# A written order for all engines, and attention products in four array quadrants, in a fused attention and gated-conv kernel

## Chip, cores and metric

The kernel runs on one NeuronCore of a Trainium2 chip. The metric is the device time of one execution in microseconds (us). Before the change the median of 3 runs is 379.87 us (379.6 to 380.04).

## What is computed

Windowed attention for 4 batches, 8 heads, 768 positions of 64 values feeds a two-layer block with a gate. In the reference, cut to what matters:

```python
k_sum = k.reshape(B, H, nb, 32, D).max(axis=3)      # 24 summary keys
v_sum = v.reshape(B, H, nb, 32, D).mean(axis=3)     # 24 summary values
scores_l = scale * q @ k.T, only where |i - j| < 16
scores_s = scale * q @ k_sum.T + log(32)
a = softmax(concat(scores_l, scores_s))
x = a @ concat(v, v_sum)                            # 4 x 768 x 512 over all heads
h = relu(x @ w_in)                                  # 512 -> 1024
conv_out = 3 taps along the sequence, per channel, of h
out = (h * sigmoid(conv_out)) @ w_out               # 1024 -> 512
```

All of it is in 32-bit floats. The two large products are made from split operands: a high part and a low part of each, three products of four (high-high, high-low, low-high).

## The kernel before

The sequence of each batch is cut into two halves, so there are 8 chunks c of 384 positions. Two heads make a pair, so a chunk has 4 pairs, and the program 32, counted n. A pair has 6 blocks of 64 queries; a block sees 96 keys of its own window and the 24 summary keys, 120 in all.

For a pair, `qk` (line 303) makes the scores: TensorE multiplies 64x64 queries with 64x120 keys, two heads in the two halves of the array's rows, two blocks in the two halves of its columns, so four run at once. `softmax` adds the mask and finds the maximum on VectorE (`masked`, 349), takes six exponentials on ScalarE (`expo`, 366), the reciprocal on VectorE (`recip`), and scales on GpSimd (`norm`). The probabilities are turned on TensorE, from pair SPLIT = 14 on by `turn_both` (417), 64 rows at a time into two PSUM banks, and copied out by ScalarE. `av` (441) multiplies 120 keys with 64 queries: the two heads stand in the two halves of the array's columns, and each takes all of its rows. A product of 32-bit floats is two matmul records, so `av` has 24. Its result in PSUM bank x is split into xh (cast by ScalarE) and xl (subtraction by VectorE, `x_lo`).

For a chunk, `f1` (538) projects x to 128 channels at a time, unit u of 8, with 12 matmuls. `relu` and `tap_mid` follow on ScalarE or VectorE (ScalarE for the chunks in TAP_ACT, VectorE for the middle taps of the others), `taps` on VectorE, `gate_tanh` on ScalarE, `gate_prod` on VectorE, `gate_hi` mostly on ScalarE, `gate_lo` on GpSimd. `f2` (641) contracts the gated channels into output tiles, three matmuls per piece; `f2_out` (667) copies a tile out on ScalarE, which also issues its store.

In the first half of a batch, each pair also needs its summaries: `key_max` and `val_sums` reduce on VectorE, `val_turn` (276) turns the sums on TensorE into bank x, `val_mean` (284) scales them on ScalarE, `load_vm` brings them behind the other values by a DMA, and `key_sums` (263) copies the summary keys behind the window on GpSimd. The tiles kw, q and va have 3, 4 and 4 buffers.

The order: chunks 0 and 1 and the pairs up to 13 follow the string ORDER, which holds on TensorE, VectorE, GpSimd and SyncE, and on ScalarE by added dependencies. From chunk 2 on `unit` (789) traces the work of one projection, and only TensorE keeps the traced order:

```python
    with tc.manual_schedule(engines={every.PE}):
        for c in range(FIRST, NCHUNK):
            pieces = work(c)
            for u in range(NFC):
                unit(c, u, pieces)
```

The framework's scheduler places the work of the other engines, and may place it ahead of the end of ORDER. In odd units, `unit` traces on TensorE the transposes of pair m-1, the scores of m and the products of m-2, then `f1`, then the pieces of `f2`; even units have `f1`, pieces, and in the first half of a batch `val_turn` ahead of them. The PSUM banks are: x; t for transposes; two banks s for scores; f2; and three for `f1`, of which one is given to the transposes at pair 15.

Of the kernel before, what the change touches and what calls it, by code (L numbers as in the profile page):

```python
# [18 lines left out]
P = 128  # L19
# [69 lines left out]
def attention_ffn(ctx, tc, qT, kT, vT, v4, w_in, cwT, w_out, mask8, ident_in, out):  # L89
# [98 lines left out]


    state = {}  # L190
    banks = ["f1a", "f1b", "f1c"]

    def f1_bank(name):
# [20 lines left out]
    def load_k(n):  # L214
        b, p = divmod(n // (2 * NP) * NP + n % NP, NP)
        tag, bufs = ("kw", 3) if 2 <= n < NP else ("kT", 2)
        k = sp.tile([P, SP], F32, tag=tag, name=f"k{n}", bufs=bufs)
        nc.sync.dma_start(k, kT[b, p])
        of(n)["k"] = k

    def load_kw(n):
        c, p = divmod(n, NP)
        b, hf = divmod(c, 2)
        first = kT[b, p, :, hf * CH : hf * CH + WK]
        nc.sync.dma_start(kw_tile(n)[:, :, :WK], window(first, 1, [SP, P], WK))

    def load_vt(n):
        c, p = divmod(n, NP)
        if c == 0:
            v = raw_b[:, 2 + p, :S].bitcast(F32)  # L230
        else:
            v = sp.tile([P, 1024], F32, tag="stage", name=f"vt{n}", bufs=2)[:, :S]
        nc.sync.dma_start(v, vT[c // 2, p])
        of(n)["vt"] = v

    def load_q(n):
        c, p = divmod(n, NP)
# [16 lines left out]
    def load_vm(n):  # L254
        nc.sync.dma_start(of(n)["va"][WK:NK, :, :], vm_wide(n))
# [37 lines left out]
    def first_half(n):  # L293
        return n // NP % 2 == 0
# [71 lines left out]
    def expo(n, h, i):  # L366
        st = of(n)
        this = nc.scalar.activation(  # L368
            st["a", h][:, i, :],
            st["a", h][:, i, :],  # L370
            AF.Exp,
            bias=st["nm"][:, h, i : i + 1],
            scale=-1.0,
            accum_out=st["acc"][:, h, i : i + 1],
        )
        before = st.setdefault("expos", [])
        if n >= NP:
            for x in before:
                tc.declare_no_dep(
                    ins(this), ins(x), reason="one engine, sums in columns of their own"  # L380
                )
        before.append(this)

    def recip(n):
        st = of(n)
# [8 lines left out]
    def softmax(n):  # L394
        for h in range(2):
            for i in range(3):
                masked(n, h, i)
            for i in range(3):
                expo(n, h, i)
        recip(n)  # L400
        for h in range(2):
            norm(n, h, "g")
# [6 lines left out]
        of(n)["pt", h] = pt  # L409

    def turned(n, h, eng):
        aT = sp.tile([P, 3 * P], F32, tag="aT", name=f"aT{n}_{h}", bufs=4)
        copy(eng, aT[:NK, :], of(n)["pt", h][:NK, : 3 * P])
        for blk in range(CB):
            of(n)["aT", h, blk] = aT[:NK, blk * QB : (blk + 1) * QB]

    def turn_both(n):
        st = of(n)
        a = [st.pop(("a", h)) for h in range(2)]
        pt = [  # L420
            ps.tile([P, 512], F32, tag=tag, name=f"pt{n}_{tag}") for tag in ("t", *given)
        ]
        for h in range(2):
            for i in range(3):
                at = (h * 3 + i) * QB
                for half in range(2):
                    r = slice(half * QB, (half + 1) * QB)
                    nc.tensor.transpose(  # L428
                        pt[half][:NK, at : at + QB], a[h][r, i, :], ident[r, r]
                    )  # L430
        for half in range(2):
            aT = sp.tile([P, 3 * P], F32, tag="aT", name=f"aT{n}_b{half}", bufs=4)
            nc.scalar.copy(aT[:NK, :], pt[half][:NK, : 3 * P])
            for h in range(2):
                for i in range(3):
                    at = (h * 3 + i) * QB
                    st["aT", h, 2 * i + half] = aT[:NK, at : at + QB]
# [3 lines left out]
    def av(n):  # L441
        st = of(n)
        xp = ps.tile([P, 512], F32, tag="x", name=f"xp{n}")
        for blk in range(CB):
            for h in range(2):
                r = slice(h * QB, (h + 1) * QB)
                nc.tensor.matmul(  # L447
                    xp[r, blk * QB : (blk + 1) * QB],
                    st["va"][:NK, blk, r],
                    st["aT", h, blk],  # L450
                    start=True,
                    stop=True,
                )
        st["xp"] = xp

    def x_tiles(c):
        xT[c] = [
# [20 lines left out]
        xh, xl = x_at(n)  # L478
        nc.vector.tensor_tensor(xl, of(n)["xp"][:, :CH], xh.bitcast(F32), ALU.subtract)  # L479

    npair = NCHUNK * NP

    def slot(j):

        if j % 2 == 0:
            n = j // 2 + 2
            if n < npair:
                if first_half(n):
                    load_k(n)
                load_kw(n)  # L490
                if first_half(n):
                    load_vt(n)
            n = j // 2
            if n < npair:
                load_vm(n)
                qk(n)
                softmax(n)
        else:
            n = (j + 1) // 2
            if n + 1 < npair:  # L500
                load_q(n + 1)
            if n < npair:
                if first_half(n):
                    val_sums(n)
                    val_turn(n)
                    val_mean(n)
                load_v(n)
                if first_half(n):
                    key_max(n)
                key_sums(n)  # L510

    def turn_one(j):
        n, h = divmod(j, 2)
        turn(n, h)
        turned(n, h, "s")

    def slot_t(j):
        if j % 2 == 0 and j - 2 < NGROUP and j // 2 - 1 >= SPLIT:
            turn_both(j // 2 - 1)

    def slot_av(j):
        n = j - 4
        if n % 2 == 0 and n < NGROUP:
            n //= 2
            c, p = divmod(n, NP)
            av(n)
            if p == 0:
                x_tiles(c)
                if c % 2:
                    x_edge(c)  # L530
            xh, xl = x_at(n)
            nc.scalar.copy(xh, of(n)["xp"][:, :CH])
            x_lo(n)


# [200 lines left out]
        mybir.DependencyClass.NoSync, mybir.DependencyReason.DATA  # L736
    )

    def run(order):
        traced = nc.cur_bb.bb.instructions  # L740
        front, behind, of_exp = [], [], None
        for token in order.split():
            what, at, eng = re.fullmatch(r"([a-zA-Z]+)([\d.]*)(?:/([svg]))?", token).groups()
            args = [int(x) for x in at.split(".") if x]
            start = len(traced)
            steps[what](*args, *([eng] if eng else []))
            for x in traced[start:]:
                if x.engine != every.Activation:
                    continue
                exp = args[0] if what == "e" else None  # L750
                if exp is None or exp != of_exp:
                    front, behind, of_exp = [], front, exp
                for y in behind:
                    tc.add_manual_dep(x, y.name, order_only, reason="order")
                front.append(x)

    with tc.manual_schedule(engines={every.PE, every.DVE, every.Pool, every.SP}):
        run(ORDER)
# [13 lines left out]
        parts = [(*t, [fc]) for t in tiles for fc in range(NFC)]  # L772
        return deal(parts, (3, 3, 2, 3, 3, 2, 4, 4))

    pending = []
    given, spare = [], [banks[0]]

    def gates(lag):

        while len(pending) > lag:  # L780
            c, fc = pending[0]
            b, hf = divmod(c, 2)
            old = (0, 1, 2) if hf == 0 else (2, 3, 4, 5)
            if b and not all((b - 1, st, fc) in contracted for st in old):
                return
            pending.pop(0)
            gate_mul(c, fc)

    def unit(c, u, pieces):

        j = 8 * (c + 1) + 3 + u
        if j == 2 * SPLIT + 2:
            given.append(banks.pop(banks.index(spare[0])))
        early = divmod(j - 2, 2)[0]
        if early < SPLIT and j % 2 == 0:
            turn_one(j - 2)
        slot_t(j)
        slot(j)
        slot_av(j)
        if early < SPLIT:  # L800
            if j % 2 == 0:
                turn_one(j - 1)
            elif u == 0:
                turn_one(j - 2)
        gates(1)
        f1(c, u, range(NCC))
        gate_conv(c, u)
        pending.append((c, u))
        assert len(pending) <= 2
        for x in pieces[u]:  # L810
            f2(*x)
        if c == NCHUNK - 1:
            gates(0)

    with tc.manual_schedule(engines={every.PE}):
        for c in range(FIRST, NCHUNK):
            pieces = work(c)
            for u in range(NFC):
                unit(c, u, pieces)

    banks += given
    for st in (2, 3, 4):
# [63 lines left out]
```

## Time and profile before

| | |
|---|---|
| median of 3 runs | 379.87 us |
| the profiled execution | 379.0 us, its span 376.9 us |
| TensorE matmuls busy | 368.7 us, 98% |
| VectorE busy | 251.7 us, 67% |
| ScalarE busy | 241.9 us, 64% |
| GpSimd busy | 145.2 us, 39% |

PE is TensorE's matmul, PEld its weight load, DVE VectorE, ACT ScalarE, POOL GpSimd. Times of rows count from the start of the span. Matmuls overlap, so a busy PE may still have room; what a matmul costs is read from the distance between starts. In a timeline a row starts with its start and its length in us, "xN" is a count of merged instructions, and brackets tell of idle time before it and what ended it.

### The profile page before, as it was taken

What the parts mean: (1) busy time and instruction counts of PE and PEld (TensorE: products, weight loads), DVE (VectorE), ACT (ScalarE), POOL (GpSimd) and SP (SyncE); (2) the same over time, 40 slices, a digit from 0 to 9 for tenths busy, and PEclk for the clock granted to TensorE, in tenths of its full rate; (3) what the DMA queues carried; (4) which work ended last, traced back from release to release, by engine and by line L of the source; (5) the groups of instructions that cost most, each with busy time, mean ns of one, the idle gap of its engine ahead of it and who ended that gap; (6) DMA issues with size and microseconds to landing.
All of it is one profiled execution on the core that took longest, in us unless ns stands there. A gap on an engine that the chain in (4) does not pass through costs nothing.

```text
span 376.9 us, 9285 instructions
## 1 busy us (share of the span) xinstructions
PE 368.7 (98%) x3407; PEld 319.6 (85%) x3407; DVE 251.7 (67%) x786; ACT 241.9 (64%) x770; POOL 145.2 (39%) x178
## 2 busy tenths in 40 slices
PE   8988999999999999999999999999999999999996
PEld 6767798888878888888888888888888988999886
DVE  3999999999877566786755655566756655565200
ACT  2999989997577677675656777665656643334211
POOL 0656577877245333423424334324323322222200
PEclk9999999999999999999999999999999999999999
DMA  7999899797974554662232442442120000000011
GB/s 288 370 330 297 230 274 319 224 248 203 277 265 149 136 161 139 175 197 72 73 103 83 121 122 85 125 115 56 64 67 3 30 28 13 16 30 28 28 57 56
DMA packets 42365, 53.27 MB, mean 141 GB/s; under 512 B 21520, under 2 KB 30160, under 8 KB 42320
## 3 DMA queue, kind: packets, MB, share of 16 engines
q1 hardware_dynamic: 38432, 46.14, 42.1%
q10 hardware_dynamic: 3888, 6.54, 4.9%
q8 instruction: 27, 0.44, 0.5%
q14 instruction: 18, 0.15, 0.2%
HBM read 44.31 MB, written 6.29 MB: 134 GB/s over the span
## 4 chain that ended last, share of the span: by engine, by line
PE 83%; DVE 8%; ACT 5%; issue 2%; DMA 1%; DVEq 0%; ACTq 0%
PE f L549 33%; PE f L654 32%; PE xp L447 5%; PE pq L318 5%; PE pw L115 2%; PE pt_t L428 2%; DVE t L590 2%; PE f L687 2%; ACT a L368 1%; DVE wu L139 1%; DMA wo<-w_out 1%; DVE wl L133 1%; PE pt L408 1%; DVE a L355 1%; ACT wu L122 1%
## 5 line engine op out<-in xcount | busy, mean ns | idle before, releaser
L629 POOL TENSOR_TENSOR glo<-t,ghi 128x383 fp32r<-128x383 f32 (+1 forms) x64 | 65.0, 1017 | 117.7 <-ACT ghi L147 108.9
L549 PE MATMUL f<-xh,win_hi 128*128 128x384 f32 (+1 forms) x256 | 92.0, 359 | 2.0 <-DVE t L611 1.9
L590 DVE SCALAR_TENSOR_TENSOR t<-f,cw,t 128x384 f32<-128x384 f32 (+3 forms) x128 | 78.4, 616 | 14.2 <-ACT t L577 10.9
L549 PE MATMUL f<-xl,win_hi 128*128 128x384 f32 (+1 forms) x256 | 86.8, 339 | 0.0
L549 PE MATMUL f<-xh,win_lo 128*128 128x384 f32 (+1 forms) x256 | 86.5, 338 | 0.0
L368 ACT ACTIVATE a<-a,nm 128x120 f32<-128x120 f32 x192 | 68.9, 400 | 9.9 <-DVE nm L355 8.7
L654 PE MATMUL f<-wout_hi,ghi 128*128 128x512 f32 x184 | 72.4, 394 | 0.0
L654 PE MATMUL f<-wout_lo,ghi 128*128 128x512 f32 x184 | 72.1, 392 | 0.0
L654 PE MATMUL f<-wout_hi,glo 128*128 128x512 f32 x184 | 71.6, 390 | 0.0
L606 ACT ACTIVATE t<-t 128x385 f32<-128x385 f32 (+1 forms) x64 | 33.7, 527 | 57.0 <-DVE t L590 56.3
L392 POOL TENSOR_TENSOR a<-a,sm 128x360 f32<-128x360 f32 x59 | 46.4, 803 | 54.9 <-DVE sm L387 52.3
L549 PEld LDWEIGHTS f<-xh,win_hi 128*128 128x128 f32 x256 | 48.2, 188 | 8.0 <-DVE t L611 3.9
L611 DVE SCALAR_TENSOR_TENSOR t<-t,f 128x383 f32<-128x383 f32 (+1 forms) x64 | 35.3, 552 | 29.4 <-ACT t L606 29.2
L549 PEld LDWEIGHTS f<-xl,win_hi 128*128 128x128 f32 x256 | 48.4, 189 | 1.4 <-DVE xl L479 0.3
L549 PEld LDWEIGHTS f<-xh,win_lo 128*128 128x128 f32 x256 | 48.3, 189 | 0.0
L355 DVE CUSTOM_DVE_ANT_0 a<-pq,mask 128x120 f32<-128x120 f32 x192 | 42.3, 277 | 3.3 <-PE pq L331 1.7
L654 PEld LDWEIGHTS f<-wout_hi,glo 128*128 128x128 f32 x184 | 34.5, 188 | 7.5
L567 ACT ACTIVATE f<-f 128x384 f32<-128x384 f32 (+1 forms) x63 | 30.8, 491 | 15.3 <-PE f L549 14.8
L654 PEld LDWEIGHTS f<-wout_hi,ghi 128*128 128x128 f32 x184 | 34.6, 188 | 5.6 <-ACT ob L669 0.3
L654 PEld LDWEIGHTS f<-wout_lo,ghi 128*128 128x128 f32 x184 | 34.6, 188 | 4.9
L368 ACT ACTIVATION_READ_ACCUMULATOR a<-a,nm 128x1 f32 x192 | 33.8, 176 | 0.0
L147 ACT CAST ghi<-t 128x383 fp32r<-128x383 f32 (+1 forms) x58 | 30.0, 517 | 5.9 <-DVE t L611 5.6
(76 smaller groups left out, 491.0 us busy)
## 6 DMA issues: line engine op xcount, KB each, us to landing
va<-v SPq DMA_DIRECT2D x32, 288.0 KB
kw<-kT SPq DMA_DIRECT2D x24, 288.0 KB
k<-kT SPq DMA_DIRECT2D x16, 400.0 KB
q<-qT SPq DMA_DIRECT2D x32, 192.0 KB
out_dram<-ob ACTq DMA_DIRECT2D x23, 256.0 KB
vt<-vT SPq DMA_DIRECT2D x12, 384.0 KB
wo<-w_out SPq DMA_DIRECT2D x8, 512.0 KB
raw_a<-w_in SPq DMA_DIRECT2D x6, 512.0 KB
```

The lines of the kernel that those rows point to most:

```text
L147: nc.scalar.copy(out, x)
L318: nc.tensor.matmul(pq[h][half * QB : (half + 1) * QB, i * NK : i * NK + keys.shape[-1]], st["q"][r, blk * QB : (blk + 1) * QB], keys, star ...
L355: nc.vector.tensor_tensor_reduce(st["a", h][:, i, :], st["pq"][h][:, i * NK : (i + 1) * NK], mask[:, edge(n, i), :], -0.125, 3.0e38, ALU.a ...
L368: this = nc.scalar.activation(st["a", h][:, i, :], st["a", h][:, i, :], AF.Exp, bias=st["nm"][:, h, i : i + 1], scale=-1.0, accum_out=st[" ...
L392: by[eng].tensor_tensor(a, a, s, ALU.mult)
L549: nc.tensor.matmul(ph[:, :n], w[:, fc, cc, :], x[:, cc, :n], start=(cc == 0 and m == 0), stop=(cc == NCC - 1 and m == 2),)
L567: nc.scalar.activation(h[:, :n], h[:, :n], AF.Relu)
L590: nc.vector.scalar_tensor_tensor(t[:, i0:i1], h[:, hf + k - 1 + i0 : hf + k - 1 + i1], cw[:, fc, k : k + 1], t[:, i0:i1], ALU.mult, ALU.add,)
L606: nc.scalar.activation(t, t, AF.Tanh, scale=0.5)
L611: nc.vector.scalar_tensor_tensor(t, t, 1.0, h[:, hf : hf + ng], ALU.add, ALU.mult)
L629: nc.gpsimd.tensor_tensor(gate_at("lo", c, fc), t, hi.bitcast(F32), ALU.subtract)
L654: nc.tensor.matmul(po, gx[:, fc, ss], w[:, fc, :], start=(fc == 0 and m == 0), stop=(fc == NFC - 1 and m == 2),)
```

## The change

From chunk 2 on `row` (odd units) and `between` (even units) write the order for TensorE, VectorE, GpSimd and SyncE, and `in_order` extends ScalarE's ordering to it. In a row TensorE now has the scores of pair m, the products of m-2, the transposes of m-1, the projection, the pieces. From pair 13 on the products are cut (`av_halves`): 64 keys go to bank x, the other 56 to free columns of three other banks, so that four products of 64x64 stand in the four quadrants of the array. ScalarE copies the first part out (`x_first`), VectorE adds the second to it (`x_sum`), GpSimd casts and subtracts. The tiles of turned probabilities have 3 buffers instead of 4. Reductions, gates and copies have fixed places. `slot`, `slot_t`, `slot_av`, `gates` and `unit` go.

```diff
+    def av_halves(n):
+        st = of(n)
+        xp = ps.tile([P, 512], F32, tag="x", name=f"xp{n}")
+        if n + 2 < npair:
+            last = of(n + 2)["pq"][1]
...
+        for blk in range(CB):
+            i, half = divmod(blk, 2)
+            if half == 0:
+                parts.append(rest[i][:, 3 * P :])
+            for k, keys in enumerate((slice(0, QB), slice(QB, NK))):
+                for h in range(2):
+                    r = slice(h * QB, (h + 1) * QB)
+                    at = blk * QB if k == 0 else half * QB
+                    nc.tensor.matmul(
+                        (parts[i] if k else xp)[r, at : at + QB],
+                        st["va"][keys, blk, r],
+                        st["aT", h, blk][keys, :],
+                        start=True,
+                        stop=True,
+                    )
+        st["x0"], st["parts"] = xp, parts
+
+    def x_first(n):
+        xs = sp.tile([P, DM], F32, tag="wl", name=f"xs{n}", bufs=1)[:, :CH]
+        nc.scalar.copy(xs, of(n)["x0"][:, :CH])
+        of(n)["xp"] = xs
+
+    def x_sum(n):
+        xs = of(n)["xp"]
+        for i, more in enumerate(of(n)["parts"]):
+            at = xs[:, i * P : (i + 1) * P]
+            nc.vector.tensor_tensor(at, at, more, ALU.add)
...
+    def x_rows(n, eng):
...
+        copy(eng, xh, of(n)["xp"][:, :CH])
+        if eng == "g":
+            nc.gpsimd.tensor_tensor(xl, of(n)["xp"], xh.bitcast(F32), ALU.subtract)
+        else:
             x_lo(n)
...
+    def row(c, u, before):
+        m = (8 * (c + 1) + 3 + u) // 2
+        new = m > SPLIT
...
+        here = m < npair
+        n = m + 2
+        if n < npair:
+            if first_half(n):
+                load_k(n)
+            load_kw(n)
+            if first_half(n):
+                load_vt(n)
+        if not new:
+            turn_one(2 * m - 2)
+        if here:
+            load_vm(m)
+            qk(m)
+        if m - 2 < npair:
+            if new:
+                av_halves(m - 2)
+            else:
+                av(m - 2)
+        if new and m - 1 < npair:
+            turn_both(m - 1)
+        gate_tanh(*before)
+        if here:
+            masks(m, 0)
+        gate_prod(*before)
+        if here:
+            masks(m, 1)
+        if new and m - 2 < npair:
+            x_first(m - 2)
+        gate_hi(*before, "s")
+        gate_lo(*before)
+        if not new:
+            x_rows(m - 2, "s")
+            turn_one(2 * m - 1)
+        if here:
+            expos(m, 0)
+            expos(m, 1)
+        if new and m - 2 < npair:
+            x_sum(m - 2)
+            x_rows(m - 2, "g")
+        if new and m - 1 < npair:
+            turned_both(m - 1)
+        if here:
+            recip(m)
+            for h in range(2):
+                norm(m, h, "g")
         f1(c, u, range(NCC))
+        relu(c, u, "s")
+        mid(c, u)
+        n = m + 1
+        if n < npair:
+            if first_half(n):
+                key_max(n)
+                val_sums(n)
+            key_sums(n)
+        taps(c, u)
+
+    def between(c, u, before):
+        m = (8 * (c + 1) + 4 + u) // 2
+        if c == FIRST and u == 0:
+            turn_one(2 * m - 3)
+            key_sums(m)
+        if m + 1 < npair:
+            load_q(m + 1)
+        if m < npair:
+            load_v(m)
+        if before:
+            gate_tanh(*before)
+            gate_prod(*before)
+        f1(c, u, range(NCC))
+        relu(c, u, "s")
+        mid(c, u)
+        if before:
+            gate_hi(*before, "s")
+            gate_lo(*before)
+        if m < npair and first_half(m):
+            val_turn(m)
+            val_mean(m)
+        taps(c, u)
+
+    before = ()
+    with tc.manual_schedule(engines={every.PE, every.DVE, every.Pool, every.SP}):
+        start = len(nc.cur_bb.bb.instructions)
         for c in range(FIRST, NCHUNK):
             pieces = work(c)
             for u in range(NFC):
-                unit(c, u, pieces)
+                (row if u % 2 else between)(c, u, before)
+                for x in pieces[u]:
+                    f2(*x)
+                before = (c, u)
+        gate_mul(*before)
+        in_order(start)
```

## Rows read from the trace of the kernel before

**Rows 1.** Busy time by stretch: PE, PEld, DVE, ACT, POOL busy, clock, DMA share, GB/s

```profile
120.00:300.00 180.00, 180.00 (x1734) 157.41 (x1733) 116.91 (x387) 119.53 (x394) 64.22 (x82) 1.00 0.36 102
```

**Rows 2.** Waits of TensorE: in total, times, longest; the first row

```profile
PE f L549 <- DVE t L611: 1.9, 3, 0.9
```

**Rows 3.** Chain that ended last, in time, from the scores of pair 22 to those of 26

```profile
196.67 0.78 PE pq L318 x24
...
200.59 2.06 PE f L654 x9
202.65 2.10 PE f L549 x12
...
239.60 0.78 PE pq L318 x24
```

**Rows 4.** PE timeline, narrow stretches of pair 22; products by line (ns min/median/max)

```profile
196.75 0.59 PE L318 MATMUL pq<-kw,q 64*64 64x120 f32 x16
...
197.16 0.28 PE L318 MATMUL pq<-kw,q 64*64 64x120 f32 x4
197.38 0.28 PE L447 MATMUL xp<-aT_b,va 120*64 120x64 f32 x2
...
197.48 0.40 PE L447 MATMUL xp<-aT_b,va 120*64 120x64 f32 x8
...
L447 PE MATMUL xp<-aT_b,va x24: 222/222/270, 197.4 to 198.1; 120*64 120x64 f32 x24
```

**Rows 5.** PE timeline in two narrow stretches: scores of 96 columns, pair 0

```profile
6.07 0.40 PE L318 MATMUL pq<-k,q 64*64 64x96 f32 x8
...
6.07 0.48 PE L318 MATMUL pq<-k,q 64*64 64x96 f32 x12
```

**Rows 6.** Masks by line (busy us, mean ns); ACT and DVE timeline, pair 22

```profile
L355 DVE CUSTOM_DVE_ANT_0 a<-pq,mask 128x120 f32<-128x120 f32 x192 | 42.3, 277 | 3.3 <-PE pq L331 1.7 <-PE pq L318 1.3
...
197.04 0.46 ACT L433 COPY aT_b<-pt_t 120x384 f32<-120x384 f32 x1
...
197.77 0.52 ACT L147 CAST ghi<-t 128x383 fp32r<-128x383 f32 x1
198.43 0.40 ACT L368 ACTIVATE a<-a,nm 128x120 f32<-128x120 f32 x1
...
200.46 0.55 ACT L532 CAST xh<-xp 128x384 fp32r<-128x384 f32 x1
...
203.40 0.52 ACT L606 ACTIVATE t<-t 128x383 f32<-128x383 f32 x1 [1.34 <-DVE t L590]
...
202.10 1.27 DVE L590 SCALAR_TENSOR_TENSOR t<-f,cw,t 128x382 f32<-128x382 f32 x2 [0.50 <-ACT t L577]
203.96 0.55 DVE L611 SCALAR_TENSOR_TENSOR t<-t,f 128x383 f32<-128x383 f32 x1 [0.59 <-ACT t L606]
```

**Rows 7.** Timeline around the end of ORDER: ACT, DVE, POOL, PE

```profile
105.13 0.48 ACT L567 ACTIVATE f<-f 128x386 f32<-128x386 f32 x1 [0.20 <-issue]
...
108.19 2.71 DVE L590 SCALAR_TENSOR_TENSOR t<-f,cw,t 128x382 f32<-128x382 f32 x5 [1.60 <-ACT t L577]
...
87.86 0.30 POOL L265 COPY kw<-ks 128x144 f32<-128x144 f32 x1
...
112.87 0.51 POOL L149 CAST ghi<-t 128x385 fp32r<-128x385 f32 x1
113.46 1.02 POOL L629 TENSOR_TENSOR glo<-t,ghi 128x385 fp32r<-128x385 f32 x1
...
109.31 0.84 PE L318 MATMUL pq<-kw,q 64*64 64x120 f32 x24
...
112.36 0.44 PE L549 MATMUL f<-xh,win_hi 128*128 128x384 f32 x1 [0.88 <-DVE t L611]
```

**Rows 8.** Groups by line: reduction of keys, copy of the value means

```profile
L260 DVE TENSOR_REDUCE ks<-k 128x24 f32<-128x768 f32 x16 | 15.1, 945 | 5.1 <-DMA k<-kT 4.6 <-POOL kw L265 0.5
...
L287 ACT ACTIVATE vm<-pv 24x128 f32<-24x128 f32 x16 | 4.0, 258 | 4.2 <-PE pv L281 4.2
```

More of the change, by code (lines that the diff above doesn't have):

```diff
@@ L190, in attention_ffn @@
     state = {}
+    of_exps = {}
     banks = ["f1a", "f1b", "f1c"]
@@ L382, in expo @@
         before.append(this)
+        of_exps[ins(this).name] = n
     def recip(n):
@@ L411, in turned @@
     def turned(n, h, eng):
-        aT = sp.tile([P, 3 * P], F32, tag="aT", name=f"aT{n}_{h}", bufs=4)
+        aT = sp.tile([P, 3 * P], F32, tag="aT", name=f"aT{n}_{h}", bufs=3)
         copy(eng, aT[:NK, :], of(n)["pt", h][:NK, : 3 * P])
@@ L415, in turned, with turned_banks @@
             of(n)["aT", h, blk] = aT[:NK, blk * QB : (blk + 1) * QB]
+    def turned_banks(n):
+        st = of(n)
+        if "pts" not in st:
+            st["pts"] = [
+                ps.tile([P, 512], F32, tag=tag, name=f"pt{n}_{tag}")
+                for tag in ("t", *given)
+            ]
+        return st["pts"]
     def turn_both(n):
@@ L419, in turn_both @@
         a = [st.pop(("a", h)) for h in range(2)]
-        pt = [
-            ps.tile([P, 512], F32, tag=tag, name=f"pt{n}_{tag}") for tag in ("t", *given)
-        ]
+        pt = turned_banks(n)
         for h in range(2):
@@ L430, in turn_both, with turned_both @@
                     )
+    def turned_both(n):
+        st = of(n)
+        pt = st["pts"]
         for half in range(2):
-            aT = sp.tile([P, 3 * P], F32, tag="aT", name=f"aT{n}_b{half}", bufs=4)
+            aT = sp.tile([P, 3 * P], F32, tag="aT", name=f"aT{n}_b{half}", bufs=3)
             nc.scalar.copy(aT[:NK, :], pt[half][:NK, : 3 * P])
@@ L454, in av @@
         st["xp"] = xp
+    def av_halves(n):
+        st = of(n)
+        xp = ps.tile([P, 512], F32, tag="x", name=f"xp{n}")
+        if n + 2 < npair:
+            last = of(n + 2)["pq"][1]
+        else:
+            last = ps.tile([P, 512], F32, tag="s", name=f"xq{n}", bufs=2)
+        if n + 1 < npair:
+            rest = [*turned_banks(n + 1), last]
+        else:
+            rest = [
+                ps.tile([P, 512], F32, tag=tag, name=f"xr{n}_{tag}")
+                for tag in ("t", *given)
+            ] + [last]
+        parts = []
+        for blk in range(CB):
[23 more added lines that the diff above has]
+            nc.vector.tensor_tensor(at, at, more, ALU.add)
+    npair = NCHUNK * NP
     def x_tiles(c):
@@ L479, in x_lo @@
         nc.vector.tensor_tensor(xl, of(n)["xp"][:, :CH], xh.bitcast(F32), ALU.subtract)
[L481 to L510, printed above, removed]
     def turn_one(j):
@@ L515, in turn_one, with masks, expos @@
         turned(n, h, "s")
[L517 to L532, printed above, removed]
+    def masks(n, h):
+        for i in range(3):
+            masked(n, h, i)
+    def expos(n, h):
+        for i in range(3):
+            expo(n, h, i)
+    def x_rows(n, eng):
+        c, p = divmod(n, NP)
+        if p == 0:
+            x_tiles(c)
+            if c % 2:
+                x_edge(c)
+        xh, xl = x_at(n)
+        copy(eng, xh, of(n)["xp"][:, :CH])
+        if eng == "g":
+            nc.gpsimd.tensor_tensor(xl, of(n)["xp"], xh.bitcast(F32), ALU.subtract)
+        else:
             x_lo(n)
@@ L737, in attention_ffn, with in_order @@
     )
+    act = {"front": [], "behind": [], "exp": None}
+    def in_order(start):
+        for x in nc.cur_bb.bb.instructions[start:]:
+            if x.engine != every.Activation:
+                continue
+            exp = of_exps.get(x.name)
+            if exp is None or exp != act["exp"]:
+                act.update(front=[], behind=act["front"], exp=exp)
+            for y in act["behind"]:
+                tc.add_manual_dep(x, y.name, order_only, reason="order")
+            act["front"].append(x)
     def run(order):
-        traced = nc.cur_bb.bb.instructions
-        front, behind, of_exp = [], [], None
         for token in order.split():
@@ L744, in run @@
             args = [int(x) for x in at.split(".") if x]
-            start = len(traced)
+            start = len(nc.cur_bb.bb.instructions)
             steps[what](*args, *([eng] if eng else []))
[L747 to L755, printed above, removed]
+            in_order(start)
     with tc.manual_schedule(engines={every.PE, every.DVE, every.Pool, every.SP}):
@@ L773, in work @@
         return deal(parts, (3, 3, 2, 3, 3, 2, 4, 4))
-    pending = []
     given, spare = [], [banks[0]]
[L778 to L792, printed above, removed]
-            given.append(banks.pop(banks.index(spare[0])))
[L794 to L805, printed above, removed]
-        f1(c, u, range(NCC))
[L807 to L813, printed above, removed]
@@ L815, in attention_ffn, with mid @@
-    with tc.manual_schedule(engines={every.PE}):
+    def mid(c, u):
+        tap_mid(c, u, "s" if c in TAP_ACT else "v")
+    def row(c, u, before):
+        m = (8 * (c + 1) + 3 + u) // 2
+        new = m > SPLIT
+        if m == SPLIT + 1:
+            given.append(banks.pop(banks.index(spare[0])))
+        here = m < npair
[14 more added lines that the diff above has]
+                av_halves(m - 2)
+            else:
+                av(m - 2)
[26 more added lines that the diff above has]
+                norm(m, h, "g")
+        f1(c, u, range(NCC))
+        relu(c, u, "s")
[7 more added lines that the diff above has]
+        taps(c, u)
@@ L816, in attention_ffn @@
+    before = ()
+    with tc.manual_schedule(engines={every.PE, every.DVE, every.Pool, every.SP}):
+        start = len(nc.cur_bb.bb.instructions)
         for c in range(FIRST, NCHUNK):
@@ L818, in attention_ffn @@
             for u in range(NFC):
-                unit(c, u, pieces)
+                (row if u % 2 else between)(c, u, before)
[3 more added lines that the diff above has]
+        gate_mul(*before)
+        in_order(start)
     banks += given
```

## The prediction

> **What bounds the kernel now.** I read the busy time by stretch first. Between 120 and 300 us, where all the pairs of chunks 3 to 7 and most of chunk 2 pass, TensorE has work in flight for all of the 180 us at a granted clock of 1.00 (the 2.4 GHz level), VectorE, ScalarE and GpSimd for 117, 120 and 64 us [rows 1]. The view of waits says the same from the other side: the largest entry of TensorE's matmuls is 1.9 us, three waits in the whole program [rows 2]. So from chunk 2 on a microsecond is gained only by giving TensorE less to do; the other engines matter only if a new order makes TensorE wait. One pair (an odd unit "row" and the even unit behind it, two projections each) takes (239.60 - 196.67) / 4 = 10.73 us [rows 3].
>
> Where could TensorE do less? The narrow stretches of its timeline show what a change of tile shape costs. Four score matmuls start together and the next four 0.103 us later ((0.59 - 0.28) / 3). The last four start at 197.16, so further ones of the same shape could start at 197.27; the first attention products, of another shape, start at 197.38. That is 0.11 us lost. Their second pair starts at 197.48, 0.10 after the first, while later pairs follow at 0.059 ((0.40 - 0.222) / 3, one matmul taking 0.222): another 0.04 [rows 4]. A switch costs 0.15 us. A pair has four today: into the transposes, the scores, the products and the projection.
>
> **The change, part by part.**
>
> *Quadrants.* Products of 64 keys and scores then have one shape, and one switch goes. The 120 keys become 64 and 56, so 24 records become 48, but four run at once instead of two: 12 fours for 12 pairs. Does a four of 64 columns keep the 0.059 us of a pair? No row has one. From the rows: fours of 120 columns take 0.103, of 96 columns 0.08 (0.48 - 0.40), which goes down to 0.054 at 64 columns; the pairs of 64 columns of today take 0.059 [rows 4, 5]. Ends: 0.054 (a gain of 12 x 0.005 x 19 = 1.1 us) and 0.08, the narrowest four that is on record (12 x 0.021 x 19 = 4.8 us lost). I take 0.059, as the columns point there and the pairs already have them: nothing gained or lost. Pairs 13 to 31 (19) go this way, of which 17 stand behind scores: 17 x 0.15 = **2.6 us gained**. Transposes last still cost one switch in and one out. They also read probabilities that have been ready for longer; TensorE did not wait for these, so that is worth nothing.
>
> *The sum of the two key parts.* ScalarE's copy replaces a cast of the same size. VectorE's subtraction becomes three additions over 128x128; the nearest row is a masked pass of 128x120 at 42.3 / 192 = 0.22, so 0.7 us. GpSimd gets a cast (0.51) and a subtraction (1.02) per pair [rows 6, 7]; with 64 of 180 us busy it has room. x of a chunk's last pair is needed some 8.5 us after its row began (2.1 until the projection, 2.1 for it, 2.8 for four pieces of output at 0.69, three quarters of the next projection [rows 3]), and I place it about 7 us after (second mask pass until 2.9, sum until 3.7, GpSimd until 5.5, a late start of 1 to 1.5). Costed at nothing; without that cover each microsecond of lateness would be paid at six chunk starts.
>
> *The written order on VectorE, GpSimd, SyncE and ScalarE.* The question is whether their loop still fits into TensorE's, now 10.73 - 0.15 = 10.58 us. Going round once: masks of one head 0.66, gate product 0.55, cast of the gate 0.4 (copies follow each other at (197.77 - 197.04) / 2), six exponentials 2.03 (198.43 to 200.46), two copies of transposes 0.73, ReLU 0.48, middle tap 0.62 (a pass like each of the two taps), two taps 1.27, tanh 0.52, then in the even unit again ReLU 0.48, middle tap 0.62, taps 1.27: 9.63, and some six crossings at 0.04 (tanh ends at 203.92, the product starts at 203.96): 9.9 us [rows 6, 7]. It fits with 0.7 to spare, so the plain pairs cost nothing. SyncE's loads keep their place relative to the pairs, one or two pairs ahead of use; the first thing that each waits for is a buffer released a pair earlier. Also nothing.
>
> *Where it does not fit: value means.* In pairs 16 to 19 and 24 to 27 VectorE also reduces keys and values, 0.95 us each, and the mean is copied out by ScalarE, now behind tanh, ReLU and cast of the even unit; it stands in bank x, which the next products need. In chunks 3 and 5 the middle tap is VectorE's too. I walked that row from its first score at 0, the taps before it ending at 0.5: masks 1.5, product 2.05, cast 2.5, exponentials 4.5, copies 5.25, ReLU 5.75, middle tap 6.4, reductions 8.3, taps 9.6, tanh 10.15, ReLU 10.65, cast 11.2, mean (0.26) 11.45. TensorE in that time: scores, products, transposes until 2.1, projection 4.2, three pieces of output 6.3, projection 8.4, turn of the values 8.5, two pieces 10.0, next scores until 10.75: it then waits 0.7 us for bank x [rows 6, 8]. Two such places: **1.4 us lost**. Ends: 0 (ScalarE 0.7 ahead of this walk) and 4.5, if every crossing costs 0.08 and each of eight pairs waits.
>
> *The seam behind the first written order.* Now VectorE stands 1.60 us with a tap of chunk 1 behind it, since a tap of chunk 2 was slipped in ahead; so TensorE stands idle for 0.88 us before the projection at 112.36. A strict order takes this away. But the summary keys of pair 14 were copied at 87.86, long ahead; now GpSimd does it behind its last two gates of chunk 1. Walked from ReLU (1,6) at 105.13: 105.6, middle tap 106.2, two taps 107.3, product (1,7) 107.85, cast 108.2 (0.35 taken, less than GpSimd's 0.51), then on GpSimd 1.02 + 0.51 + 1.02 + 0.30 = 111.05; up to 0.5 less, as ScalarE no longer has hoisted copies there. Pair 14's scores then start at 110.6 to 111.1 instead of 109.31, and the projection behind them 2.1 later, as now without the idle time: 112.7 to 113.2 against 112.36 [rows 7]. I take **0.3 us lost**, by the earlier start. Ends: 0.9 gained (the copy not in the way) and 4.5 lost (GpSimd's tail as late as now, its last subtraction ending at 114.48 and the copy at 114.8).
>
> **Sum:** -2.6 + 1.4 + 0.3 = -0.9 us. The profiled execution took 379.0 (span 376.9 and 2.1 around it), so 378.1; the median of the runs shown is 0.9 above the profiled one: **379.0**. What a measurement can tell from no change is about 0.2%, 0.76 us.
>
> **Rivals.**
> *Clean (0.20):* no wait for bank x and the copy of pair 14 out of the way: -2.6 - 0.9 = -3.5, 376.4. For it: ScalarE is idle a third of the time. Against: its order is fixed, and idle time before tanh cannot be used.
> *The loop becomes the bound (0.17), slower:* the place is the chain masks, gate, exponentials, copies, ReLU, taps. It decides from 10.58 us a round on. Twelve steps and crossings each 0.07 longer, as GpSimd's 1.5 us more could cause by slowing VectorE, make 10.8: 17 x 0.22 = 3.7 us more, 382.7. Against it: 0.7 us of spare room.
> *Quadrants keep the pace of the 96-column fours (0.06):* 4.8 more, 383.8.
> *A floor on matmul starts (0.03).* Scores of 96 columns start every 0.02 us on average, four within 0.08 [rows 5]; at 0.025 a start, 48 records would take 1.2 us instead of 0.7, 19 x 0.5 = 9.5 more, 388.5. The Trainium skill states such a floor (TensorE: Matmul & The Clock Gate, "Wait — 56ns, not 53.3ns?": starts never less than about 25 ns apart, however few the columns); the rows above contradict it, which is why its chance is small.
> *The switch stays (0.04):* scores and products would still be 0.15 further apart than need be, by a wait for a semaphore: 2.6 more, 381.6.
>
> **How the numbers follow.** The forecast has 0.50, its own range 377.4 to 380.2: 0.30 of it faster by over 0.2%, 0.16 within, 0.04 slower. With the clean case faster has 0.50. Within has 0.18, as half of the chance that the switch stays goes with other gains. Slower has 0.04, loop, slow quadrants, floor and the other half: 0.32. The range 376.0 to 383.0 takes in clean and loop; it leaves out the slow quadrants, the floor and the worst ends of seam and loop.
>
> **What would show it.** Right: in each pair the first product about 0.10 us after the last four scores began, 48 records in some 0.7 us; the pair's period near 10.58; TensorE waiting for ScalarE's vm in two places for 0.5 to 1 us; the scores of pair 14 near 110.8, released by GpSimd's copy. Wrong: products of 0.9 us or more; TensorE waiting in most pairs for the gate product, for bank x or for probabilities; a period over 10.73.

## The result: 1.0% faster, and the profile after

The median of 4 runs is 376.13 us (375.48 to 376.81) against 379.96 us for the kernel before (4 runs): a ratio of 0.9901, 95% interval 0.9878 to 0.9924. The profiled execution took 376.61 us, its span 374.8.

The page of the kernel after, its first lines; "x" counts instructions:

```profile
span 374.8 us, 10298 instructions
## 1 busy us (share of the span) xinstructions
PE 365.8 (98%) x3863; PEld 319.9 (85%) x3863; DVE 253.6 (68%) x824; ACT 241.8 (65%) x770; POOL 170.7 (46%) x216
```

GpSimd took over the x operands, 25.5 us more than the 145.2 of before. TensorE is still the bound. The busy time by stretch answers to [rows 1]:

```profile
120.00:300.00 180.00, 179.11 (x2097) 158.41 (x2086) 122.03 (x427) 119.36 (x394) 87.61 (x119) 1.00 0.41 117
```

The clock is 1.00 as before (the 2.4 GHz level), but 0.89 us in 180 are now idle, where there were none. The view of TensorE's waits says for what (in total, times, longest):

```profile
PE pw L115 <- DVE idle L110: 1.1, 1, 1.1
PE pv L282 <- DVE vs L272: 1.0, 1, 1.0
PE xp L492 <- ACT vm L288: 0.9, 2, 0.4
PE f L579 <- DVE t L641: 0.6, 2, 0.3
```

The first two lie in the part that the change leaves alone. The third is new: products wait twice for ScalarE's value means. The fourth is what is left of the 1.9 us of [rows 2].

**The pair.** The chain in order of time answers to [rows 3]:

```profile
194.33 0.78 PE pq L319 x24
196.30 2.29 PE f L579 x12
198.59 2.06 PE f L684 x9
200.65 2.10 PE f L579 x12
...
236.68 0.78 PE pq L319 x24
```

Four pairs take 42.35 us instead of 42.93: 0.145 less a pair. The narrow TensorE timeline of pair 22, for [rows 4], shows where:

```profile
194.26 0.85 PE L319 MATMUL pq<-kw,q 64*64 64x120 f32 x24
...
194.62 0.49 PE L319 MATMUL pq<-kw,q 64*64 64x120 f32 x12
...
194.93 0.21 PE L492 MATMUL xp<-aT_b,va 64*64 64x64 f32 x1
...
194.98 0.22 PE L492 MATMUL xp<-aT_b,va 64*64 64x64 f32 x1
...
195.04 0.22 PE L492 MATMUL xp<-aT_b,va 64*64 64x64 f32 x1
...
195.59 0.22 PE L492 MATMUL pq<-aT_b,va 56*64 56x64 f32 x1
195.74 0.27 PE L437 MATMUL pt_t<-ident,a 64*120 64x64 f32 x1
```

The last three fours of scores begin from 194.62 on, 0.103 apart, so the last at 194.83; the first products begin at 194.93, 0.10 later, as a further four of scores would. The 0.11 us of dead time of [rows 4] are gone. The 48 products begin within 0.66 us, twelve fours 0.059 apart.

**The seam.** The timeline around the end of ORDER, of GpSimd, VectorE and TensorE, for [rows 7]:

```profile
88.63 0.30 POOL L266 COPY kw<-ks 128x144 f32<-128x144 f32 x1
...
105.34 1.27 DVE L620 SCALAR_TENSOR_TENSOR t<-f,cw,t 128x385 f32<-128x385 f32 x2 [0.55 <-ACT t L607]
106.53 0.55 DVE L641 SCALAR_TENSOR_TENSOR t<-t,f 128x385 f32<-128x385 f32 x1
...
108.88 0.85 PE L319 MATMUL pq<-kw,q 64*64 64x120 f32 x24
...
110.80 0.42 PE L579 MATMUL f<-xh,win_hi 128*128 128x384 f32 x1
```

VectorE takes the last taps of chunk 1 after 0.55 us instead of 1.60, and the projection behind the scores starts at 110.80, with no idle time, instead of 112.36. Counted from the scores of pair 14, which differ by 0.43 us between the two profiles, that is 1.92 us instead of 3.05. And the summary keys of pair 14 are copied at 88.63, twenty microseconds ahead of need: the strict order did not hold them back.

**Bank x.** TensorE's and ScalarE's timelines at the first wait (the second, at 247.93, is alike):

```profile
160.63 0.53 ACT L636 ACTIVATE t<-t 128x385 f32<-128x385 f32 x1 [3.59 <-DVE t L620]
161.06 0.48 ACT L597 ACTIVATE f<-f 128x386 f32<-128x386 f32 x1
161.78 0.51 ACT L147 CAST ghi<-t 128x385 fp32r<-128x385 f32 x1 [0.24 <-DVE t L641]
162.20 0.26 ACT L288 ACTIVATE vm<-pv 24x128 f32<-24x128 f32 x1
...
161.58 0.49 PE L319 MATMUL pq<-kw,q 64*64 64x120 f32 x12
162.51 0.32 PE L492 MATMUL xp<-aT_b,va 64*64 64x64 f32 x3 [0.45 <-ACT vm L288]
```

The means stand behind tanh, ReLU and cast, just as they were walked in the prediction. The two rows concerned take 11.29 and 11.30 us where they took 10.67 and 10.68.

### The profile page after: what moved, and what is told of

Same layout as the page of the kernel before. It is cut to its first block, busy times and chain, and to the rows that moved or that the text cites. A ratio compares the mean times of both kernels' runs of the same rounds, so it can differ in the third digit from the quotient of the medians.

```text
span 374.8 us, 10298 instructions
## 1 busy us (share of the span) xinstructions
PE 365.8 (98%) x3863; PEld 319.9 (85%) x3863; DVE 253.6 (68%) x824; ACT 241.8 (65%) x770; POOL 170.7 (46%) x216
## 4 chain that ended last, share of the span: by engine, by line
PE 75%; DVE 11%; DMA 8%; ACT 3%; issue 1%; SPq 1%; DVEq 0%; ACTq 0%
PE f L684 31%; PE f L579 30%; DMA raw_a<-w_in 4%; PE pq L319 4%; PE xp L492 3%; DMA cw_words<-cwT 2%; DVE t L620 2%; PE pt_t L437 2%; DVE wu L139 2%; PE f L717 2%; DMA vt<-vT 1%; PE pt L410 1%; PE xp L460 1%; DVE wl L133 1%; ACT a L369 1%
## 5 line engine op out<-in xcount | busy, mean ns | idle before, releaser
L620 DVE SCALAR_TENSOR_TENSOR t<-f,cw,t 128x382 f32<-128x382 f32 (+3 forms) x128 | 78.7, 616 | 11.2 <-ACT t L607 7.7
L636 ACT ACTIVATE t<-t 128x383 f32<-128x383 f32 (+1 forms) x64 | 33.7, 526 | 63.5 <-DVE t L620 62.7
L356 DVE CUSTOM_DVE_ANT_0 a<-pq,mask 128x120 f32<-128x120 f32 x192 | 43.5, 276 | 6.3 <-PE pq L319 4.6
L609 DVE TENSOR_SCALAR t<-f,cw 128x385 f32<-128x385 f32 (+1 forms) x35 | 21.6, 617 | 20.7 <-ACT f L597 18.9
```

What stands on the lines that cost most here:

```text
L356: nc.vector.tensor_tensor_reduce(st["a", h][:, i, :], st["pq"][h][:, i * NK : (i + 1) * NK], mask[:, edge(n, i), :], -0.125, 3.0e38, ALU.a ...
L609: nc.vector.tensor_scalar(t, h[:, hf : hf + ng], cw[:, fc, 1:2], 1.0, ALU.mult, ALU.mult)
L620: nc.vector.scalar_tensor_tensor(t[:, i0:i1], h[:, hf + k - 1 + i0 : hf + k - 1 + i1], cw[:, fc, k : k + 1], t[:, i0:i1], ALU.mult, ALU.add,)
L636: nc.scalar.activation(t, t, AF.Tanh, scale=0.5)
```

## The experiments

Each was timed beside the kernel before on the same chip (380.17, 380.0, 380.14 and 379.55 us on the four chips). One execution differs from the next mostly ahead of pair 14: in the profiles of one and the same first order, its scores start between 108.1 and 110.3 us, with waits of 0 to 1.8 us for loads of queries there. In four of the profiles (the kernel after again, transposes between, TensorE's order only, one more copy), behind such a wait of 1.5 us or more, the granted clock was also at its 1.2 GHz level for 3.4 us, between 42 and 47 us. So beside the median I give the stretch from the start of the scores of pair 14 to that of the last projection's last matmul, which two profiles of the kernel after have as 237.26 and 237.29. In the kernel before the change it is 239.29.

**The kernel after again.** No edit.

> The changed kernel again, as the base for the others on this chip. Theory: 376 us, 0.99 of the kernel before; one pair 10.60 us where no value mean is made, two waits of TensorE for the value mean's copy (vm) of about 0.45 us idle each.

376.45 us, ratio 0.990 [0.9878, 0.9923], stretch 237.29.

**Means early: is the wait for bank x what it costs?**

```diff
         gate_tanh(*before)
         gate_prod(*before)
     f1(c, u, range(NCC))
+    if m < npair and first_half(m):
+        val_turn(m)
+        val_mean(m)
     relu(c, u, "s")
     mid(c, u)
     ...
-    if m < npair and first_half(m):
-        val_turn(m)
-        val_mean(m)
     taps(c, u)
```

> Turn and copy of the value mean stand right behind the projection, ahead of ReLU on ScalarE. Theory (bank x is held by the mean's copy, which waits behind ReLU and the gate's cast): the periods of 11.29 and 11.30 us in chunks 3 and 5 become 10.5 to 10.6, both waits of TensorE for vm go, 1.4 us less than the changed kernel. Rival (these two rows are late by the reductions, whatever stands in bank x): the waits return under another name, within 0.3 us of the changed kernel.

374.53 us, 0.986 [0.983, 0.9891]; stretch 235.70, 1.56 less than after. TensorE's waits, the first rows:

```profile
PE pw L115 <- DVE idle L110: 1.1, 1, 1.1
PE pv L282 <- DVE vs L272: 1.0, 1, 1.0
PE f L579 <- DVE t L641: 0.8, 1, 0.8
```

The wait for vm is gone, and the two rows fall to 10.53 and 10.52 us. The theory holds, and this is the fastest version of the study.

**Whole keys: what are the quadrants worth?** The products stay behind the scores and the transposes last, but a product takes all 120 keys.

```diff
-            if new:
-                av_halves(m - 2)
-            else:
-                av(m - 2)
+            av(m - 2)
+            of(m - 2)["x0"], of(m - 2)["parts"] = of(m - 2)["xp"], []
```

> The products take all 120 keys at once again, two at a time, in the same place behind the scores; nothing is left to sum on VectorE. Theory (the gain in a pair is one switch of tile shape, 0.15 us): pairs take 0.15 us longer, 17 x 0.15 = 2.5 us more than the changed kernel. Rival (the gain comes from the written order alone): the same time as the changed kernel. Second rival (four quadrants also multiply faster): over 3.5 us more.

378.64 us, 0.9961 [0.9942, 0.9981]; stretch 239.40, 2.1 more than after. A plain pair takes 10.77 us instead of the 10.60 of after; the chain, for pair 23:

```profile
204.74 0.78 PE pq L319 x24
...
215.51 0.78 PE pq L319 x24
```

The switch between scores and products is back, at some 0.16 a pair.

**Transposes between scores and products: is it the shape or the number of matmuls?** The quadrants stay, but stand behind another shape.

```diff
+            if new and m - 1 < npair:
+                turn_both(m - 1)
             if new:
                 av_halves(m - 2)
             ...
-        if new and m - 1 < npair:
+        elif new and m - 1 < npair:
             turn_both(m - 1)
```

> Quadrants and sums stay, but the transposes stand between scores and products, so that a switch of shape more is needed. Theory (the switch is all the gain): 17 x 0.15 = 2.5 us more than the changed kernel, products still 0.66 us. Rival (four quadrants are worth it by themselves): under 1 us more.

378.99 us, 0.997 [0.9953, 0.9986]; stretch 239.36, and the same pair takes 10.77:

```profile
206.49 0.78 PE pq L319 x24
...
217.26 0.78 PE pq L319 x24
```

So quadrants alone give nothing; they pay only where they follow the scores. (The two waits for bank x shrink here, rows of 10.53 and 10.78, as the products come later; the whole of what the extra switch costs is thus somewhat more than 2.1.)

**Only TensorE's order written.**

```diff
-    with tc.manual_schedule(engines={every.PE, every.DVE, every.Pool, every.SP}):
+    with tc.manual_schedule(engines={every.PE}):
     ...
-        in_order(start)
```

> The same traced steps, but from chunk 2 on only TensorE keeps the written order, as before the change; the scheduler places VectorE, ScalarE, GpSimd and SyncE. Theory (the written order gains at the end of ORDER, about 1.5 us, and loses at the value means, about 1.5 us): within 1 us of the changed kernel, with the wait ahead of the second projection of chunk 2 back and no waits for vm. Rival (without the written order the longer way of x is late at chunk starts and in most pairs): over 2 us more than the changed kernel.

387.77 us, 1.0198 [1.017, 1.0226], stretch 246.62. The theory missed the time by far, and the rival held for another reason than a late x. (Of the theory's two details one came out: the wait of 0.9 us ahead of the second projection of chunk 2 is back; one wait for vm, 0.4 us, is left.) TensorE's waits, first row:

```profile
PE f L684 <- ACT ob L699: 6.4, 8, 1.5
```

Eight times the output product waits until ScalarE has emptied its single bank f2. Unordered, ScalarE's output copies come late.

**ScalarE's order kept, the others free.** The same edit without taking `in_order(start)` away.

> The changed kernel with the written order on TensorE and ScalarE alone; VectorE, GpSimd and SyncE are placed by the scheduler. Theory (with TensorE's order alone the time went to waits for the copy of the output tile on ScalarE, so ScalarE's order is what counts): within 2 us of the changed kernel. Rival (all engines are needed): 5 us or more above the changed kernel.

377.89 us, 0.9951 [0.9931, 0.9971]; stretch 236.48, even 0.8 less than after. Of the four added orders, ScalarE's is the one that this kernel can't do without in this stretch; with it the projection starts 1.92 us behind the scores of pair 14, as with all orders written. The 0.8 us are one wait for vm less: the rows of pairs 19 and 27 take 10.53 us instead of 11.3, and that of pair 16, with the one wait left, 11.37 instead of 10.60. The 1.4 us that the median is above that of after lie ahead of the stretch: the scores of pair 14 start at 111.14 here, with 2.7 us of waits for loads before them, and with 3.4 us at the 1.2 GHz level of the clock from 24.5 on. One profile can't say whether the free order of SyncE's loads does that every time; the section on the prediction has an estimate over all executions (at "The sum").

**The summary keys of pair 14 held behind ORDER on GpSimd,** as the prediction had assumed.

```diff
+            tail = [x for x in nc.cur_bb.bb.instructions if x.engine == every.Pool][-1]
+            begin = len(nc.cur_bb.bb.instructions)
             key_sums(m)
+            for x in nc.cur_bb.bb.instructions[begin:]:
+                if x.engine == every.Pool:
+                    tc.add_manual_dep(x, tail.name, order_only, reason="order")
```

> The copy of pair 14's summary keys is held behind the last gate of chunk 1 on GpSimd, where the prediction had it. Theory (the prediction failed there only in the place): the copy runs near 110.1 to 110.4, the scores of pair 14 start near 110.5 instead of 108.9, 1.5 us more than the changed kernel. Rival (TensorE makes it up later): within 0.3 us of the changed kernel.

377.85 us, 0.9942 [0.9921, 0.9964]. TensorE's timeline:

```profile
110.69 0.85 PE L319 MATMUL pq<-kw,q 64*64 64x120 f32 x24 [1.43 <-POOL kw L266]
```

That is the predicted seam: scores "at 110.6 to 111.1", released by GpSimd, and 1.4 us on the median.

**How much room has the loop?** The means early, and ScalarE's copy of x made twice, then four times.

```diff
-        nc.scalar.copy(xs, of(n)["x0"][:, :CH])
+        for _ in range(2):
+            nc.scalar.copy(xs, of(n)["x0"][:, :CH])
```

> On the kernel with the early mean: ScalarE copies the first part of x twice in every pair, some 0.4 us more in the loop of the other engines. Theory (the loop of 9.9 us has 0.7 us of room): less than 0.5 us more than the kernel with the early mean. Rival (that loop is the bound): 17 x 0.4 = 6.8 us more.

376.54 us, 0.9912 [0.9887, 0.9938]; stretch 236.94, 1.24 more than with the means early alone. Plain pairs don't change (10.6 us). Two rows in which value sums are turned take 10.39 us instead of 10.03, with TensorE waiting for the sums; two others, in which a new output tile begins in bank f2, take 10.79 instead of 10.54. For these the profile names no wait; the next run shows one at that place.

> As before with four copies in place of one, some 1.2 us more in the loop. Theory (9.9 + 1.2 = 11.1 us against 10.58 of TensorE): up to 17 x 0.5 = 8.5 us more than the kernel with the early mean, less the lateness that the buffers take up, so 3 to 9 us. Rival (ScalarE is idle a third of the time, so that it can take 1.2 us of 10.6): less than 1 us more.

389.15 us, 1.0239 [1.0201, 1.0278]; stretch 248.89, 13.2 more, beyond what was expected. TensorE's waits:

```profile
PE pv L282 <- DVE vs L272: 6.2, 5, 1.3
PE f L685 <- ACT ob L700: 4.7, 3, 2.0
...
PE pv L282 <- ACT ob L700: 1.2, 1, 1.2
```

Three copies are some 1.5 us of ScalarE a pair. Many plain pairs still keep their period (10.53, 11.21, 9.8), while others take up to 12.87. What gives way is not the whole loop's length, but single places: the turn of the values, which needs VectorE's sums, and the bank f2.

**x on ScalarE and VectorE instead of GpSimd,** the means early.

```diff
         x_sum(m - 2)
-        x_rows(m - 2, "g")
+        x_rows(m - 2, "s")
```

> On the kernel with the early mean: the cast of the summed x goes to ScalarE and its low part to VectorE instead of GpSimd, 0.4 us and 0.5 us more in their loop. Theory (only the rows with value means have no room, as with one more copy): 1 to 2.5 us more than the kernel with the early mean, all of it in waits for the value sums or the outputs' copy. Rival (the loop has room everywhere): less than 0.5 us more.

379.51 us, 0.9982 [0.9963, 1.0001]; stretch 240.32, 4.6 more than with the means early, where 1 to 2.5 were expected. TensorE's waits, the first and the third row:

```profile
PE pv L282 <- DVE vs L272: 3.0, 5, 1.0
...
PE f L684 <- ACT ob L699: 1.2, 2, 0.6
```

The same two places. The move to GpSimd is what pays for the sum of the key parts; without it the quadrants' gain is gone.

**The written order alone:** whole keys, and x by ScalarE's cast straight from bank x and VectorE's subtraction, as before.

```diff
-            if new:
-                av_halves(m - 2)
-            else:
-                av(m - 2)
+            av(m - 2)
             ...
-            x_first(m - 2)
+            x_rows(m - 2, "s")
             ...
-        if new and m - 2 < npair:
-            x_sum(m - 2)
-            x_rows(m - 2, "g")
```

> The written order without the quadrants: products of 120 keys behind the scores, x cast by ScalarE out of bank x and the low part taken by VectorE, as before the change. Theory (order: 1.5 us gained at the end of ORDER and 1.5 lost at the value means; quadrants: 2.5): about 378.5 us, 0.996 of the kernel before, as with whole keys and GpSimd. Rival (the way of x over GpSimd is needed to keep ScalarE and VectorE in time): over 380 us.

378.46 us, 0.996 [0.9944, 0.9976]; stretch 239.33, and the two waits for the means are there (0.9 us in total). So the median of the change divides into 1.7 us from the order, net of those waits, and 2.0 from the quadrants. (The two kernels were timed on different chips, each against the kernel before.) In the stretch the order gives nothing (239.33 against 239.29): what the seam gains there, the waits take.

**Means early, and only TensorE's and ScalarE's order written.** This was to tell whether the 0.8 us above came from the wait for the means alone. The edit took the engines' set from both written blocks, so that VectorE, GpSimd and SyncE were free in ORDER too, which the expectation doesn't speak of.

```diff
-    with tc.manual_schedule(engines={every.PE, every.DVE, every.Pool, every.SP}):
+    with tc.manual_schedule(engines={every.PE}):
         run(ORDER)
     ...
-    with tc.manual_schedule(engines={every.PE, every.DVE, every.Pool, every.SP}):
+    with tc.manual_schedule(engines={every.PE}):
```

> The value means issued ahead of ReLU, and only TensorE's and ScalarE's order written, the other engines left to the scheduler. Theory: the order of VectorE, GpSimd and SyncE has no part in the gain, and what the run without it had less from the scores of pair 14 to the last projection (0.8 us) was the wait for the value means alone, which this kernel has not either way: that stretch comes out where it was with the means early, 235.7 +- 0.3 us, and the median at 374.5 to 376.5, by how late the first written order ends. Rival: the free order of VectorE and GpSimd gives something of its own, 0.8 us: the stretch comes out near 234.9. Second rival: it costs, a late x or a late gate in some pairs: 236.2 or more, with a wait of TensorE named.

387.97 us, 1.0197 [1.0161, 1.0233]. The scores of pair 14 start at 122.66 us instead of 108.08: 14.6 us are lost in ORDER, where the granted clock was 0.83 in the first 60 us, against 1.00 with the means early: 20.5 of the 60 us were at the 1.2 GHz level, the longest part from 15.3 to 32.4, behind a wait of 1.45 us for GpSimd's scaling. At half the clock 20.5 us can cost at most some 10 of the 14.6. The busy time by stretch, columns as in [rows 1], its first rows:

```profile
0.00:60.00 60.00, 52.96 (x575) 41.25 (x575) 44.50 (x148) 39.05 (x131) 27.52 (x33) 0.83 0.80 259
60.00:100.00 40.00, 38.95 (x375) 33.88 (x374) 35.73 (x117) 37.04 (x120) 27.18 (x31) 1.00 0.79 241
```

The median therefore says nothing of the theories. The stretch does, with care: 236.08, above the 235.4 to 236.0 of the theory and below the 236.2 of the second rival, far from the 234.9 of the first. A free order of VectorE and GpSimd gave nothing of its own here; with the means early, the written one is 0.4 us shorter.

## Why the prediction was right, and where it was not

The forecast was 379.0 in a range of 376.0 to 383.0, and faster was the likeliest. The time came out 2.9 us lower, only 0.13 us inside the range and next to the rival called clean (376.4), but by other terms. That it still lies in the range is luck: the seam, put down as a loss, was a gain, and an earlier end of ORDER, which no term of the sum holds, gave some 1.7 us by an estimate (see "The sum").

**The switch: right.** 17 x 0.15 = 2.6 was predicted. The period falls by 0.145 on the mean of the 14 pairs from 15 to 30 that have no vm wait, which makes 2.5 us for 17; taking the shape neighbours apart in two ways cost 2.1 each.

**The pace of the quadrants: right.** A four takes 0.059 us as chosen, neither 0.054 nor the 0.08 of the 96-column fours.

**Value means: right.** Two waits of 0.7 us in chunks 3 and 5 were predicted; in pairs 17 and 25 the products start some 0.7 us after the last four scores, where 0.10 would do, released by vm (pair 17: 161.58 + 2 x 0.103 = 161.79 to 162.51). They cost 0.77 each against a clean row (11.30 - 10.53); moving the means away gave back 1.6.

**The seam: wrong, with the wrong sign.** The step that failed is "now GpSimd does it behind its last two gates of chunk 1". I took the new written order to follow the old one on GpSimd. It is a block of its own, and the copy is the first GpSimd instruction in it that waits for nothing late; it ran at 88.63, as at 87.86 before. What was right in that part is the other half: the strict order takes away the slipped tap and with it the idle time before the projection. Instead of 0.3 lost, the projection started 1.56 earlier (112.36 to 110.80): 1.13 by the seam (3.05 to 1.92 behind the scores; 1.92 or 1.93 in every profile in which ScalarE's order is written on, 3.06 in the one with TensorE's order only), and 0.43 by an earlier start of the scores, which varies from one execution to the next. Holding the copy back gave the scores at 110.69 and cost 1.4 us, so the price of the wait was right and its presence wrong.

**The loop: right for plain pairs, too generous for the others.** "It fits with 0.7 to spare" held for plain pairs: one more copy on ScalarE, 0.5 us, left them alone. In four rows, at two turns of value sums and two new output tiles, the same copy cost 1.24 us altogether. The spare room belongs to each handover, not to the loop. What the rival of the loop needed, a VectorE slowed by GpSimd's added work, did not show: a tap took 616 ns on the mean before and after.

**x on GpSimd: right, with more room than walked.** The timeline of VectorE and GpSimd in the row that starts at 194.26:

```profile
197.24 0.28 DVE L510 TENSOR_TENSOR xs<-xs,pq 128x128 f32<-128x128 f32 x1
...
197.90 0.51 POOL L149 CAST xh<-xs 128x384 fp32r<-128x384 f32 x1
198.49 0.86 POOL L561 TENSOR_TENSOR xl<-xs,xh 128x384 fp32r<-128x384 f32 x1
```

x is complete at 199.35, 5.1 us after the row began; the prediction had 7, and a need at 8.5. For the last pairs of the chunks, of which it spoke, it is 5.1 to 5.3. The three additions run 0.20 apart, 0.7 us together, as taken.

**The sum: a term was missing.** In the stretch, -2.5 (switch) - 1.13 (seam) + 1.54 (means) = -2.1 us, and it is 2.03 shorter. With the 0.43 by which the scores of pair 14 start earlier, the last projection's last matmul starts at 346.14 instead of 348.60. The two profiled executions differ by 2.4 us. The medians differ by 3.8; the profiled execution of before was 0.9 to 1.0 under its median and that of after 0.5 above its own. So 1.4 us of the median's difference are not placed in these two profiles.

An estimate places most of them ahead of pair 14. The stretch hardly varies (237.26, 237.29, and 237.26 with the summary keys held). So the start of pair 14's scores follows for every execution from its span, less the stretch and what comes behind it in the profile (28.3 and 28.7 us; other profiles have 28.2 to 28.7, so the result is uncertain by about 0.5). At the median this gives 108.7 us for the kernel after (10 executions) and 110.35 for the kernel before (73, timed beside the experiments); the profile of before, with 109.31, was an early one. So ORDER ends some 1.7 us earlier, which is about what the order alone gave. The prediction put the end of ORDER at no change except at the seam.

Why it ends earlier is not shown. In the kernel before, SyncE issues 96 loads ahead of the scores of pair 14, in the kernel after 89. The two other kernels that leave SyncE free from chunk 2 on only (TensorE's order only; TensorE's and ScalarE's) issue 96 and 97 and start those scores late too, at 110.8 and 111.3 by the same estimate. No run frees SyncE alone.

## What to carry to other kernels

Count the changes of tile shape on a busy TensorE. Read as in [rows 4], those around pair 22 of the kernel after cost 0.14 us (from the output's pieces to the scores), 0.16 (products to transposes) and 0.20 (transposes to the projection). Cutting a product into the shape of its neighbour removes one at no price in matmul time. Before a strict order is put on a busy engine, list the PSUM banks that have one buffer and are emptied by it; the lateness shows there, long before the loop as a whole is full. And check what a written block is chained to: where it isn't tied to the block ahead, its first instructions may run long before that block's end.

## What the runs showed of the hardware that was not expected

48 products in four quadrants begin within 0.66 us, one every 14 ns on the mean, and twelve fours 0.059 us apart. The Trainium skill (TensorE: Matmul & The Clock Gate, "Wait — 56ns, not 53.3ns?") says that starts never come closer than about 25 ns; these rows, at a clock of 1.00, show them closer where matmuls go to different quadrants. By that rule the kernel would have been slower than before.

GpSimd's subtraction for x has one size, 128x384, but two durations. Its row in the kernel after (ns, min/median/max):

```profile
L561 POOL TENSOR_TENSOR xl<-xs,xh x19: 861/867/1023, 123.2 to 313.4; 128x384 fp32r<-128x384 f32 x19
```

In the eleven pairs of chunks 3, 5 and 7 it took 0.86 to 0.87 us, in the eight of chunks 4 and 6 1.01 to 1.02, as long as the subtraction for the gate (1.02 in [rows 7]). In the program the two kinds of chunk differ in where xh and xl begin in their tiles, two columns further in odd chunks. That this is the cause was not tried.
